# Gated attention mix on one core: score ring of four banks, GpSimd takes sums and reciprocals of branch B, DMA turns the output tiles

## The chip, the cores and the metric

The kernel runs on one core of a Trainium2 chip. A core has a matrix engine (TensorE, PE in the profile), a vector engine (VectorE, DVE), a scalar engine (ScalarE, ACT), a general engine (GpSimd, POOL), a queue engine for transfers (SyncE, SP) and 16 DMA engines. Each engine runs its own list of instructions in order and waits for the others through semaphores. SBUF is the working memory of 128 partitions. PSUM has eight banks, each 128 partitions by 512 fp32 values; matmuls write there. The metric is device microseconds from start to end of one execution.

## The reference

The kernel computes softmax attention A and a linear attention B over the same input of 2048 tokens and 512 features, 32 heads of 16, and mixes them by a gate for each token:

```python
g = sigmoid((x * gate_w).sum(-1, keepdims=True))
# A: softmax attention
scores = einsum("bhqd,bhkd->bhqk", q, k) * 16 ** -0.5
a = reshape(einsum("bhqk,bhkd->bhqd", softmax(scores), v)) @ A_wo
# B: linear attention; q, k, v from B_wqkv
phi(t) = concat([softmax(t @ w_phi), softmax(-(t @ w_phi))])
kv = einsum("bhsf,bhsd->bhfd", phi(k), v);  z = phi(k).sum(s)
b = reshape(phi(q) @ kv / (phi(q) @ z + 1e-6)) @ B_wo
out = g * a + (1 - g) * b
```

All arrays are bf16. The exponentials of A are the bulk: 32 x 2048 x 2048 scores.

## The kernel before

**Tiles.** The scores of A are cut into 2048 tiles (units) of 128 keys by 512 queries of one head. A pack is the same 128 keys for four heads, in the four row strips of PE's array (32 rows each), so four score matmuls can run beside each other. 16 packs make a group: four heads against all keys for one query chunk. Eight groups make a query chunk, and there are four chunks: 32 groups, 512 packs.

**Two ways to take the exponential.** Most units go to ACT (`_exp`, line 978): the score matmuls (`_qk`, `_scores`, line 931) write to a ring of PSUM banks, and one ACTIVATE takes the exponential of several neighbouring banks into slots of the SBUF tensor ET. The ring has `NRING` = 5 banks, used in groups of three and two in turn (`GROUPS`). ET has `NSLOT` = 25 slots. The other units, 452 of 2048, go to DVE (`_vector_batch`): a tile's scores get one of the free PSUM banks, a DVE instruction (line 847) turns them into the bits of an approximate exponential, and in batches of four tiles two further instructions (line 864, on two and on four thousand elements a partition) add constants to the bits, which makes four terms whose sum is a better approximation. `NUMS` says how many units of each of the 32 groups go this way.

**Values.** `_pv` (line 1034) multiplies the exponentials by the values, four heads in four column strips of the array, and adds them up in a PSUM accumulator, one bank for a group; a vector tile needs four such matmuls, one for each term. A column of ones among the values gives the softmax's sum. `_fill` (line 1041) adds matmuls with zero weights that keep the array busy.

**The norm of A.** When a group is complete, `_norm` transposes the accumulator on DVE (line 1055). For each pair of groups it multiplies the sums by the gate (line 1062), takes reciprocals (1064), multiplies on POOL (1067) and transposes back on DVE (1072) into `onTA`, which the output matmuls read. The last two groups are treated one at a time, on DVE alone.

**Branch B.** `_b_pair` handles two tiles of 128 tokens, eight times for keys and eight for queries: project, copy to SBUF, negate (line 1179), a max tree (1181, 1182), subtract (1184), exponential on ACT (1187), a tree of sums (1189 to 1192), reciprocal (1200), multiply (1194). All but the exponential run on DVE. DMA transposes from SP (lines 1243 and 1276) turn the results.

**PSUM.** Five banks belong to the score ring; the other three serve everything else: the accumulators, the projections, the scores of vector tiles, the outputs.

**The order.** Nothing of the order is left to run time. `Plan.order` is a list scheduler in Python: it goes through all operations with an assumed cost for each (`c_act`, `c_dve`, `c_pe` and constants), an assumed delay from one engine to another (`LAT`, `MORE`), the free PSUM banks and due times counted in packs (`prio`, `rel`, `QDUE`, `KDUE`, `VDUE`, `K0`, `SK`, `Q0`, `SQ`, `NDUE`), and writes one list for each engine. `_late` keeps PE from starting other work that would make the next scores late. `rank` puts an operation whose `urgent` time has come first. `port` makes operations that are named in `PORT` and all POOL operations follow one another in the plan; on the chip there is no such wait. `emit` writes the lists with the semaphore waits. So an instruction that is late on the chip holds up whatever stands behind it on its engine.

The lines that a sentence does not say:

```python
GROUPS = (3, 2)
...
deps=self.qks[-1:] + ([self.exps[k - 2]] if k >= 2 else ...     # _qk: two groups back must be read
...
self.ET[:, a % NS:a % NS + n, cols], self.ps[:, a % NR:a % NR + n, cols], ACT.Exp, scale=SCALE   # _exp
```

Of the kernel before, what the change touches and what calls it, by code (L numbers as in the profile page):

```python
# [39 lines left out]
class Op:  # L40
    def __init__(self, eng, fn, cost, name, prio, rel, kind, lat):
        self.eng, self.fn, self.cost, self.name = eng, fn, cost, name
        self.prio, self.rel, self.kind, self.lat = prio, rel, kind, lat
        self.deps = []
        self.users = []
        self.left = 0
        self.need = False
        self.acquire = None
        self.release = None
        self.sem = None  # L50
        self.start = self.end = None
        self.on_commit = None
        self.array = 0.0
        self.filler = 0
        self.pad = False
        self.filled = 0
        self.strips = None
        self.urgent = 1 << 30
        self.held = self.port = False
        self.alone = -99  # L60
        self.group = None


class Plan:
# [3 lines left out]
    MORE = {("ACT", "PE"): 0.09, ("ACT", "DVE"): 0.1, ("DVE", "PE"): 0.022}  # L68
    ENGS = ("PE", "ACT", "DVE", "POOL", "SP")
    LAT = {"PE": 0.215, "ACT": 0.16, "DVE": 0.12, "POOL": 0.12, "SP": 2.2}  # L70
    SWITCH, PASS, STEP = 0.105, 0.2155, 0.004
    SPAN, SHARE, FILL = 2.4, 0.5, 0.2155
    PAD, PADS, OVER = 0.45, 2, 0.2
    SLIP, GAPS, FLOOR = 0, 0.6, 0.44

    def __init__(self):
        self.ops = []
        self.now = -1
        self.free_banks = []
        self.keep = None  # L80
        self.open = None
        self.pad = None
        self.mode = None
        self.strip = [0.0] * 4
        self.n_qk, self.qks, self.exps = 0, (), ()
        self.n_acc = 0
        self.todo = {}
# [19 lines left out]
    def op(self, eng, fn, cost, reads=(), writes=(), deps=(), name="", prio=0.0, rel=-99, kind="full",  # L107
           acquire=None, release=None, lat=None, array=None, strips=None):
# [20 lines left out]
        o.acquire, o.release = acquire, release  # L129
# [7 lines left out]
    def _late(self, end):  # L137

        k = self.n_qk
        if k < 2 or k >= len(self.qks) or any(d.end is None for d in self.qks[k].deps):  # L140
            return False
# [9 lines left out]
    NEAR = 0.2  # L151
    SAME = 16
    OPEN = 99
    HURRY, FREE = 20, 60
    PORT = ("v_step", "b_neg", "b_max", "b_sub", "b_sum", "b_mul", "n_mul", "n_den", "kvbd")
# [30 lines left out]
    def _bank_for(self, o):  # L186

        if o.group is not None and self.todo.get(o.group - 1, 0) > self.OPEN:
            return False
        return len(self.free_banks) > (self.n_acc < 2 and self.keep is not None and self.keep is not o.acquire)  # L190

    def order(self):
# [14 lines left out]
        while left:  # L207
# [74 lines left out]
            if o.acquire is not None:  # L282
                k = min(range(len(self.free_banks)), key=lambda i: self.free_banks[i][1])
                bank, _, ops = self.free_banks.pop(k)
                o.acquire.bank = bank
                o.deps.extend(ops)
            if o.release is not None:
                self.free_banks.append((o.release.bank, self._seen(o, "PE"), [o]))
# [94 lines left out]
class _Kernel:  # L383
    NRING = 5
    GROUPS = (3, 2)
    NSLOT = 25
# [3 lines left out]
    NA, NST, LEAD = 2, 2, 8  # L390
    KEEP = 15
    URGENT, AHEAD, SOON, REST = 5, -(1 << 30), 4, 6
    QDUE, KDUE, VDUE = 24, 17, 8
    P_Q, P_MUL, P_NEG = 1, 1, 0
    GDUE = 26
    VMIN = 12
    ALONE, EARLY = 9, 8
    PVP = 8
# [29 lines left out]
    def _memory(self, ctx):  # L428
# [13 lines left out]
        self.iden = sb("iden", [P, P], BF16)  # L442
# [3 lines left out]
        self.zero = sb("zero", [P, 32], BF16)  # L446
        self.warm = sb("warm", [P, QCH], BF16)
        self.gwb = sb("gwb", [P, 4, P], BF16)
        self.gh = sb("gh", [P, 2, NQC, 16], F32)
# [20 lines left out]
        self.bq = sb("bq", [P, self.NBQ, 2, 2 * D], BF16)  # L470
        self.btree = sb("btree", [P, 32, 8, 4], BF16)
        self.bsum = sb("bsum", [P, P], F32)
        self.brec = sb("brec", [P, P], FP16)
        self.kvacc = sb("kvacc", [P, 2, 260], F32)
# [8 lines left out]
        tiles = [sb(f"vs{k}", [P, 2, 4, QCH], U16) for k in range(self.NST + self.NA)]  # L483
# [5 lines left out]
    def c_act(n):  # L489
        return 0.050 + n * 0.000834  # L490
# [55 lines left out]
    def _consts(self):  # L546
# [25 lines left out]
        op("POOL", lambda e: e.memset(self.zero[:], 0.0), 0.1, writes=[self.b_zero], prio=-75)  # L572
        self.b_wphi0 = B()
# [14 lines left out]
    def _projections(self):  # L588
# [8 lines left out]
        self.b_rinv, self.b_T2 = B(), B()  # L597
        self._warm(9, None)
        op("ACT", lambda e: e.activation(self.bsum[:, 0:1], self.warm[:, 0:1], ACT.Exp), 1.5, reads=[self.b_warm],
           name="table", prio=-48)  # L600
        for j in range(NQC):
            if j == 0:
                for half, banks in enumerate(((3, 4), (None, None))):
# [69 lines left out]
    def _proj_k0(self, half, bank):  # L673
# [4 lines left out]
                   self.c_dve(256), 2 * half - 2.5, -99, "kproj", [self.b_k0[half]], n=256, bank=bank)  # L678

    def _proj_q0(self, half, bank):  # L680
# [4 lines left out]
        for c in range(4):  # L685
# [3 lines left out]
                   acquire=None if c else pool)  # L689
        for side in range(2):  # L690
# [48 lines left out]
    def _proj_v(self, pr, t0):  # L739
# [5 lines left out]
        for tt in range(2):  # L745
# [8 lines left out]
            mm.urgent = 64 * pr + t0 - self.SOON + 2  # L754
# [53 lines left out]
    NUMS = (4, 10, 12, 14, 14, 14, 14, 14, 14, 14, 14, 14, 15, 14, 16, 14, 13, 14, 15, 14, 17, 14, 15, 15, 14, 14, 11, 15, 21, 16, 21, 12)  # L808

    def _plan_vector(self):  # L810
# [5 lines left out]
        batches = [away[k:k + 4] for k in range(0, len(away), 4)]  # L816
# [18 lines left out]
    def _vector_batch(self, number, units, due):  # L835
# [4 lines left out]
        parts, war = [], list(b_va.readers)  # L840
        for j, u in enumerate(units):
# [5 lines left out]
            parts.append(op("DVE", lambda e, j=j, job=job: e.tensor_scalar(  # L847
                va[:, 0, j, :], self._bank(job), SCALE * LOG2E * 128.0, float(ORIGIN), op0=ALU.mult, op1=ALU.add),
                self.c_dve(512), deps=[m] + war, name="v_bits", prio=at, release=job))
            m.urgent = parts[-1].urgent = u // 4 - self.AHEAD  # L850
# [3 lines left out]
            m.on_commit = lambda _, g=g: self.plan.todo.update({g: self.plan.todo[g] - 1})  # L854
        self.last_bits = parts
# [4 lines left out]
        for k in range(4):  # L860
# [9 lines left out]
            for g in sorted({u // (4 * NT) for u in units}):  # L870
# [4 lines left out]
                def run(e, g=g, src=src, ot=ot, v=v, tile=tile):  # L875
                    for j, u in src:
                        ins = self._values(e, ot, g % 8, u // 4 % NT, {u % 4: tile[:, j, :].bitcast(BF16)}, v)
# [8 lines left out]
    def _attention(self):  # L886
# [14 lines left out]
        self.n_step = 0  # L901
        first = sum(self.GROUPS)
# [40 lines left out]
    def _qk(self, a, b, half=None):  # L943
        plan, NR = self.plan, self.NRING
        units = self.mine[a:b]
        cols = slice(0, QCH) if half is None else slice(256 * half, 256 * half + 256)

        def run(e):
            for _ in range(o.filled):
                e.matmul(self.ps[:, a % NR, :], self.kT[:, 0, 0:P], self.kT[:, 0, 0:QCH], start=True, stop=True)  # L950
# [15 lines left out]
        o.pad = k >= 8  # L966
# [18 lines left out]
    def _pv(self, p):  # L985
# [32 lines left out]
        self.pvs.append(o)  # L1018
        if kt == 0:
# [30 lines left out]
    def _norm(self, qc, src, side, last, dst, b_dst, due, job, alone=False):  # L1050
# [6 lines left out]
        if not (side or alone):  # L1057
# [4 lines left out]
        op("DVE", lambda e: e.tensor_tensor(rinv[:, lo:hi], den, h, ALU.mult), 0.23, reads=reads + [self.b_g],  # L1062
           writes=[b_rinv], name="n_den", prio=due)
        op("DVE", lambda e: e.reciprocal(rinv[:, lo:hi], rinv[:, lo:hi]), 0.2 + 0.1 * n, reads=[b_rinv],  # L1064
           writes=[b_rinv], name="n_rec", prio=due)
        spare = self.P_MUL and n == 2
        op("POOL" if spare else "DVE", lambda e: e.tensor_tensor(  # L1067
# [3 lines left out]
        if side == 1:  # L1071
# [4 lines left out]
    NDUE = 26  # L1076
    K0, SK, Q0, SQ = 34.0, 12.0, 214.0, 14.25

    def _branch_b(self):
# [7 lines left out]
        self.b_kvbd, self.b_onB, self.b_rinvB = B(), [B(), B()], [B(), B()]  # L1087
        self.b_phiT = [B() for _ in range(4)]
# [58 lines left out]
    def _b_pair(self, s, t0, due):  # L1147
# [25 lines left out]
        def chain(ops, off, bufs):  # L1173
            for name, cost, fn in ops:
                spare = self.P_NEG and name == "b_neg"
                op("POOL" if spare else "DVE", fn, 1.35 if spare else cost, reads=bufs, writes=bufs, name=name,
                   prio=due + off)
        spread = lambda t: t[:, :, None, :].to_broadcast([P, 32, DH, 4])
        chain([("b_neg", 0.16 + 1024 * 0.00027, lambda e: e.tensor_scalar(both[:, :, 1], both[:, :, 0], -1.0, 0.0,
                                                                         op0=ALU.mult, op1=ALU.add)),  # L1180
# [6 lines left out]
        op("ACT", lambda e: e.activation(flat, flat, ACT.Exp), 1.8, reads=[b], writes=[b],  # L1187
# [3 lines left out]
                                                                       half[:, :, n:2 * n], ALU.add)) for n in (4, 2)]  # L1191
              + [("b_sum", 0.3, lambda e: e.tensor_tensor(last(self.bsum[:]), half[:, :, 0], half[:, :, 1], ALU.add)),
                 ("b_rec", 0.96, self._b_rec),
                 ("b_mul", two(2048), lambda e: e.tensor_tensor(x, x, spread(last(self.brec[:])), ALU.mult))],  # L1194
              2, [b, self.b_tree])
        return slot

    def _b_rec(self, e):
        with self.nc.allow_low_precision(reason="11 bits, each product is rounded to 8"):
            return e.reciprocal(self.brec[:], self.bsum[:])  # L1200
# [47 lines left out]
    def _b_num(self, t, due):  # L1248
# [4 lines left out]
        b_rinv.readers = []  # L1253
        for hf in range(2):
            job = Job()

            def mm(e, hf=hf, job=job):
# [6 lines left out]
            view = self._view17(job)  # L1264
            r = rinv[:, 16 * hf:16 * hf + 16]
# [7 lines left out]
                prio=due - 20, release=job))  # L1273
        b_rinv.readers = list(muls)
# [26 lines left out]
    def _out(self, qc):  # L1301
        op, NT, NQC = self.plan.op, self.NT, self.NQC
        for tt in range(4):
# [5 lines left out]
            if final:  # L1309
                due = self.NPACK  # L1310
                deps = (self.last_bits if tt < 2 else [self.pvs[-1]]) + [w for b in b_onTA[:3] for w in b.writers]
            else:
                deps = [w for b in b_onTA for w in b.writers]
            for x in first:
                x.prio, x.rel = due, due - (6 if not final else 8 if tt < 2 else 0)
                x.deps += deps
            m = first[-1]
# [58 lines left out]
```

## Time and profile before

| | |
|---|---|
| time, median of 3 runs | 772.5 us (772.28 to 772.59) |
| the profiled execution | 772.22 us, its span 770.2 us |
| busy: PE, DVE, ACT, POOL | 747.0, 725.3, 755.1, 57.9 us |
| ACTIVATE of line 978 | 641 (318 of three tiles, 318 of two, five shorter) |
| bits of vector tiles (line 847), steps (line 864) | 452, 226 |
| granted TensorE clock | 1.0 throughout |

The span runs from the first to the last instruction; some 2 us of the time lie around it. A busy share is an average over the span. A group's line names the source line, the engine, the operation, the tile it writes and the one it reads with their sizes, the count, then busy time and mean duration, then the idle time of the engine just before these instructions and what ended it. The chain that ended last goes back from the last instruction, at each step to what released it or to the instruction before it on its engine; in order of time it gives start, length and the number of instructions of a stretch. In the view by time, PE and PEld are matmuls and their weight loads.

### The profile page before, as it was taken

What the parts mean: (1) busy time and instruction counts of PE and PEld (TensorE: products, weight loads), DVE (VectorE), ACT (ScalarE), POOL (GpSimd) and SP (SyncE); (2) the same over time, 40 slices, a digit from 0 to 9 for tenths busy, and PEclk for the clock granted to TensorE, in tenths of its full rate; (3) what the DMA queues carried; (4) which work ended last, traced back from release to release, by engine and by line L of the source; (5) the groups of instructions that cost most, each with busy time, mean ns of one, the idle gap of its engine ahead of it and who ended that gap; (6) DMA issues with size and microseconds to landing.
All of it is one profiled execution on the core that took longest, in us unless ns stands there. A gap on an engine that the chain in (4) does not pass through costs nothing.

```text
span 770.2 us, 16369 instructions
## 1 busy us (share of the span) xinstructions
PE 747.0 (97%) x7126; PEld 231.5 (30%) x7126; DVE 725.3 (94%) x1207; ACT 755.1 (98%) x663; POOL 57.9 (8%) x73
## 2 busy tenths in 40 slices
PE   8999999999999999999999999999999999999998
PEld 4333333322322232222232223222323232322222
DVE  4789999999999999999999999999999999999994
ACT  6999999999999999999999999999999999999996
POOL 3200102000010100001001010000010101010000
PEclk9999999999999999999999999999999999999999
DMA  9510000000000000000111010102001110100000
GB/s 233 124 29 1 2 1 2 1 1 2 1 1 2 1 2 1 1 2 1 29 28 29 21 35 15 42 9 49 8 9 36 32 31 16 35 9 2 1 2 28
DMA packets 46456, 16.79 MB, mean 22 GB/s; under 512 B 40752, under 2 KB 45872, under 8 KB 46384
## 3 DMA queue, kind: packets, MB, share of 16 engines
q1 hardware_dynamic: 44512, 14.97, 9.1%
q8 instruction: 55, 0.90, 0.5%
q10 hardware_dynamic: 1872, 0.79, 0.4%
q14 instruction: 17, 0.14, 0.1%
HBM read 4.21 MB, written 2.10 MB: 8 GB/s over the span
## 4 chain that ended last, share of the span: by engine, by line
ACT 87%; PE 7%; DVE 5%; DMA 1%; SPq 0%; issue 0%
ACT ET L978 83%; ACT bq L1187 4%; PE ps L931 2%; PE ps L1034 2%; PE ps L640 2%; DVE vs L847 2%; DVE vs L864 1%; DMA xT<-in_A_x_dram 1%; DVE WB L1133 0%; DVE bq L1184 0%; PE ps L1041 0%; DVE bq L1160 0%; DVE btree L1182 0%; PE ps L749 0%; DVE ghB L802 0%; SPq L515 0%
## 5 line engine op out<-in xcount | busy, mean ns | idle before, releaser
L978 ACT ACTIVATE ET<-ps 128x1024 bf16<-128x1024 f32 (+2 forms) x641 | 725.7, 1340 | 2.4 <-PE ps L931 2.4
L931 PE MATMUL ps<-qT,kT 32*128 32x512 bf16 (+1 forms) x2053 | 304.9, 383 | 12.8 <-ACT ET L978 8.2
L847 DVE TENSOR_SCALAR vs<-ps 128x512 uint16<-128x512 f32 x452 | 297.4, 681 | 13.6 <-PE ps L931 11.9
L864 DVE TENSOR_SCALAR vs<-vs 128x2048 uint16<-128x2048 uint16 x226 | 214.8, 955 | 0.8
L1034 PE MATMUL ps<-ET,V 128*32 128x512 bf16 x1596 | 196.7, 387 | 0.1
L1034 PE MATMUL ps<-vs,V 128*32 128x512 bf16 x1808 | 179.9, 384 | 2.9 <-DVE vs L864 2.7
L931 PEld LDWEIGHTS ps<-qT,kT 32*128 32x128 bf16 x2053 | 76.9, 91 | 261.0 <-ACT ET L978 187.1
L1034 PEld LDWEIGHTS ps<-ET,V 128*32 128x32 bf16 x1596 | 49.9, 94 | 92.6 <-issue 79.7
L1041 PE MATMUL ps<-kT,zero 128*32 128x512 bf16 x760 | 75.1, 383 | 0.0
L1034 PEld LDWEIGHTS ps<-vs,V 128*32 128x32 bf16 x1808 | 45.1, 95 | 67.7 <-issue 31.3
L640 PE MATMUL ps<-WB,xT 128*128 128x512 bf16 x192 | 56.7, 384 | 0.4 <-DVE WB L1133 0.4
L728 POOL TENSOR_SCALAR qT<-qtmp,mask 128x512 bf16<-128x512 bf16 x30 | 25.6, 865 | 311.2 <-DVE qtmp L723 311.2
L1067 POOL TENSOR_TENSOR T<-T,rinv 128x512 bf16<-128x512 f32 x15 | 16.5, 1102 | 296.7 <-DVE rinv L1064 296.7
L640 PE MATMUL ps<-xT,WA 128*128 128x512 bf16 x120 | 35.8, 384 | 0.0
L1187 ACT ACTIVATE bq<-bq 128x2048 bf16<-128x2048 bf16 x16 | 31.5, 1970 | 0.4 <-DVE bq L1184 0.3
L1055 DVE STREAM_TRANSPOSE T<-ps 128x512 f32<-128x512 f32 x32 | 22.7, 710 | 7.7 <-PE ps L1034 7.2
L1041 PEld LDWEIGHTS ps<-kT,zero 128*32 128x32 bf16 x760 | 19.4, 95 | 18.9 <-issue 13.7
L1160 DVE CAST bq<-ps 128x512 bf16<-128x512 f32 x32 | 21.7, 683 | 2.2 <-PE ps L640 2.2
L640 PEld LDWEIGHTS ps<-WB,xT 128*128 128x128 bf16 x192 | 14.1, 97 | 27.3 <-issue 16.4
L1184 DVE TENSOR_TENSOR bq<-bq,btree 128x2048 bf16<-128x2048 bf16 x16 | 19.8, 1240 | 0.1
L1194 DVE TENSOR_TENSOR bq<-bq,brec 128x2048 bf16<-128x2048 bf16 x16 | 19.6, 1224 | 0.0
L640 PE MATMUL ps<-WoA,onTA 128*128 128x512 bf16 x64 | 18.7, 382 | 0.0
(75 smaller groups left out, 341.2 us busy)
## 6 DMA issues: line engine op xcount, KB each, us to landing
WB<-in_B_wqkv_dram SPq DMA_DIRECT2D x1, 1536.0 KB, 8.7
out_dram<-WB SPq DMA_DIRECT2D x12, 128.0 KB, 1.7
WA<-in_A_wqkv_dram SPq DMA_DIRECT2D x2, 384.0 KB, 4.5
WoB<-in_B_wo_dram SPq DMA_DIRECT2D x1, 512.0 KB, 3.8
WoA<-in_A_wo_dram SPq DMA_DIRECT2D x1, 512.0 KB, 4.8
WA<-in_A_wqkv_dram ACTq DMA_DIRECT2D x2, 128.0 KB, 3.0
WA<-in_A_wqkv_dram ACTq DMA_DIRECT2D x1, 256.0 KB, 4.2
WA<-in_A_wqkv_dram SPq DMA_DIRECT2D x1, 256.0 KB, 5.0
```

Of the source, the lines that this page charges most:

```text
L640: return e.matmul(out, lhs, rhs, start=start, stop=stop)
L728: x = self.plan.op("POOL", lambda e, side=side: e.tensor_scalar(self.qT[:, s0 + side, :], tmp, self.mask[:, side:side + 1], 0.0, op0=ALU.m ...
L847: parts.append(op("DVE", lambda e, j=j, job=job: e.tensor_scalar(va[:, 0, j, :], self._bank(job), SCALE * LOG2E * 128.0, float(ORIGIN), op ...
L864: o = op("DVE", lambda e, k=k, src=src, dst=dst: e.tensor_scalar(dst, src, float(STEPS[k - 1]), None, op0=ALU.add), 0.16 + k * n * QCH * 0 ...
L931: return e.matmul(out[:, cols], self.kT[32 * i:32 * i + 32, cp, kt * TOK:(kt + 1) * TOK], self.qT[32 * i:32 * i + 32, s, cols], start=True ...
L978: o = plan.op("ACT", lambda e: e.activation(self.ET[:, a % NS:a % NS + n, cols], self.ps[:, a % NR:a % NR + n, cols], ACT.Exp, scale=SCALE ...
L1034: ins = e.matmul(self._bank(ot)[32 * i:32 * i + 32, :], v[:, v0:v0 + 32], tile, start=(kt == 0), stop=(kt == self.NT - 1), tile_position=( ...
L1041: ins = e.matmul(self._bank(ot)[32 * i:32 * i + 32, :], self.zero[:], self.kT[:, 0, 0:QCH], start=False, stop=False, tile_position=(0, 32 ...
L1055: t1 = op("DVE", lambda e: e.transpose(T1[:, side].rearrange("p b s -> p (b s)"), src()), 0.735, deps=last, writes=[b_T1[side]], name="n_t ...
L1160: [lambda e, b, k=k: e.tensor_copy(bq[:, k].rearrange("p (g s v) -> p g s v", g=8, s=2)[:, :, 0, :], b.rearrange("p (g v) -> p g v", g=8))],
L1184: + [("b_sub", two(2048), lambda e: e.tensor_tensor(x, x, spread(tree[:, :, 0]), ALU.subtract))],
L1187: op("ACT", lambda e: e.activation(flat, flat, ACT.Exp), 1.8, reads=[b], writes=[b], name="b_exp", prio=due + 1)
```

## The change

The diff touches constants of the plan, `_norm`, `_b_pair` and several helpers. What it does:

- The score ring has four banks and every group two tiles. Four PSUM banks are free for the rest. ET has 24 slots.
- 481 instead of 452 units go to DVE, from pack 4 on (`VMIN`) instead of 12.
- In `_b_pair` the negation, the last two steps of the tree of sums, the total and the reciprocal run on POOL. In `_norm` the reciprocal of a pair could also go there, but `P_REC` is 0, so that it stays on DVE. The new function `_reciprocal` is seven POOL instructions: a first guess from the bits, and two steps of two products and one linear term each.
- In `_norm`, the transpose back of a pair becomes 16 small SBUF to SBUF copies and one DMA transpose, all from SP, through the new tensor T3. The last two groups keep the DVE transpose.
- The plan's costs and delays change: the exponential's cost is 0.0634 + n x 0.000833 us, delays from ACT are shorter, and many due times move. First keys and queries become urgent ahead of the value projections, pads start at the second group, and the last four value products are exempt from `_late`.
- New options that stay off as the constants are set: `PAIRS` (two vector tiles in one instruction), `P_REC`, `P_M` and `P_BMUL` (further work on POOL).

```diff
-    MORE = {("ACT", "PE"): 0.09, ("ACT", "DVE"): 0.1, ("DVE", "PE"): 0.022}
+    MORE = {('ACT', 'PE'): 0.04, ('DVE', 'PE'): 0.022, ('PE', 'DVE'): 0.027}
-    LAT = {"PE": 0.215, "ACT": 0.16, "DVE": 0.12, "POOL": 0.12, "SP": 2.2}
+    LAT = {"PE": 0.215, "ACT": 0.157, "DVE": 0.12, "POOL": 0.12, "SP": 2.2}
-    SPAN, SHARE, FILL = 2.4, 0.5, 0.2155
-    PAD, PADS, OVER = 0.45, 2, 0.2
-    SLIP, GAPS, FLOOR = 0, 0.6, 0.44
+    SPAN, SHARE, FILL = 2.7, 0.5, 0.2155
+    PAD, PADS, OVER = 0.45, 2, 0
+    SLIP, GAPS, FLOOR = 0, 0.7, 0.5
...
-    NEAR = 0.2
-    SAME = 16
-    OPEN = 99
-    HURRY, FREE = 20, 60
+    TAIL = 0.0
+    NEAR = 0.1
+    SAME = 100
+    OPEN = 2
+    HURRY, FREE = 15, 30
...
-    NRING = 5
-    GROUPS = (3, 2)
-    NSLOT = 25
+    NRING = 4
+    GROUPS = (2, 2)
+    NSLOT = 24
+    PACK, PAIRS, PAIR0 = 4, 0, 0
...
-    NA, NST, LEAD = 2, 2, 8
+    NA, NST, LEAD = 2, 2, 6
-    QDUE, KDUE, VDUE = 24, 17, 8
-    P_Q, P_MUL, P_NEG = 1, 1, 0
+    QDUE, KDUE, VDUE = 28, 17, 11
+    P_Q, P_MUL, P_NEG = 1, 1, 1
+    P_REC, P_SUM = 0, 4
+    P_BACK = 1
+    P_M, P_BMUL, CHUNKS = 0, 0, 2
-    VMIN = 12
-    ALONE, EARLY = 9, 8
-    PVP = 8
+    VMIN = 4
+    FAST = 4
+    VSOON = -2
+    PADK = 2
+    ALONE, EARLY = 12, 6
+    PVP = 10
...
-        return 0.050 + n * 0.000834
+        return 0.0634 + n * 0.000833
...
-                   self.c_dve(256), 2 * half - 2.5, -99, "kproj", [self.b_k0[half]], n=256, bank=bank)
+                   self.c_dve(256), 2 * half - 2.5, -99, "kproj", [self.b_k0[half]], n=256, bank=bank,
+                   urgent=3 * half - 99)
...
-        if side == 1:
+        if side == 1 and not alone and self.P_BACK:
+            parts = [lambda e, i=i, c=c: e.dma_start(
+                self.T3[32 * c:32 * c + 32, :, 32 * i:32 * i + 32],
+                T2[32 * i:32 * i + 32].rearrange("p (b c) f -> p c b f", c=4)[:, c]) for i in range(4) for c in range(4)]
+            self.dma("SP", f"mix{due}", parts, cost=0.55 * 16, reads=[b_T2], writes=[self.b_T3], prio=due, lat=2.2)
+            self.dma("SP", f"back{due}", lambda e: e.dma_start(dst.rearrange("p (b t) -> p b t", b=4),
+                                                               self.T3[:].rearrange("p b f -> p (b f)"), transpose=True),
+                     cost=0.6, reads=[self.b_T3], writes=[b_dst], prio=due, lat=3.0)
+        elif side == 1:
...
-    K0, SK, Q0, SQ = 34.0, 12.0, 214.0, 14.25
+    K0, SK, Q0, SQ = 30.0, 11.5, 214.0, 14.5
...
+    def _reciprocal(self, s, guess, tmp, out, reads, bufs, prio):
...
+        do("r_bits", 0.17 + 0.001 * n, lambda e: e.tensor_scalar(
+            high(guess), high(s), -1.0, float(0x7EE0), op0=ALU.mult, op1=ALU.add))
+        for x, y, by, plus in ((guess, r, -1.2011100358638287, 2.192845599791731), (r, out, -1.0, 2.0)):
+            do("r_mul", 0.17 + 0.0019 * n, lambda e, x=x: e.tensor_tensor(t, s, x, ALU.mult))
+            do("r_rest", 0.17 + 0.001 * n, lambda e, by=by, plus=plus: e.tensor_scalar(
+                t, t, by, plus, op0=ALU.mult, op1=ALU.add))
+            do("r_step", 0.17 + 0.0019 * n, lambda e, x=x, y=y: e.tensor_tensor(y, x, t, ALU.mult))
```

## The prediction

> **What bounds the kernel now.** I read the page first (busy time, then the chain that ended last), next the groups by form, next that chain in order of time, and at the end the instructions in two short windows.
>
> ```profile
> PE 747.0 (97%) x7126; PEld 231.5 (30%) x7126; DVE 725.3 (94%) x1207; ACT 755.1 (98%) x663; POOL 57.9 (8%) x73
> ACT 87%; PE 7%; DVE 5%; DMA 1%; SPq 0%; issue 0%
> ```
>
> Three engines look full, but 87% of the chain that sets the end is ACT, nearly all of it the exponential of line 978. PE's figure is soft: a matmul's end is modelled. POOL is nearly empty.
>
> ```profile
> L978 ACT ACTIVATE ET<-ps 128x1536 bf16<-128x1536 f32 x318 | 494.5, 1555 | 0.4 <-PE ps L931 0.3
> L978 ACT ACTIVATE ET<-ps 128x1024 bf16<-128x1024 f32 x318 | 360.8, 1134 | 1.5 <-PE ps L931 1.5
> L847 DVE TENSOR_SCALAR vs<-ps 128x512 uint16<-128x512 f32 x452 | 297.4, 681 | 13.6 <-PE ps L931 11.9
> L864 DVE TENSOR_SCALAR vs<-vs 128x4096 uint16<-128x4096 uint16 x113 | 138.6, 1228 | 0.3
> L864 DVE TENSOR_SCALAR vs<-vs 128x2048 uint16<-128x2048 uint16 x113 | 76.7, 683 | 0.5
> L1041 PE MATMUL ps<-kT,zero 128*32 128x512 bf16 x760 | 75.1, 383 | 0.0
> L728 POOL TENSOR_SCALAR qT<-qtmp,mask 128x512 bf16<-128x512 bf16 x30 | 25.6, 865 | 311.2 <-DVE qtmp L723 311.2
> L1067 POOL TENSOR_TENSOR T<-T,rinv 128x512 bf16<-128x512 f32 x15 | 16.5, 1102 | 296.7 <-DVE rinv L1064 296.7
> L1200 DVE RECIPROCAL brec<-bsum 128x128 f16<-128x128 f32 x16 | 15.1, 945 | 0.1
> L1072 DVE STREAM_TRANSPOSE onTA<-T 128x512 bf16<-128x512 bf16 x16 | 11.2, 701 | 0.0
> ```
>
> The idle time ahead of the 636 full groups is 1.9 us in all: ACT is fed. Neighbouring exponentials overlap, so their mean durations (1555, 1134 ns) overstate them. Their true rate is in the chain:
>
> ```profile
> 481.02 39.76 ACT ET L978 x35
> ...
> 650.07 97.19 ACT ET L978 x86
> ```
>
> 86 instructions are 43 pairs (three tiles, two tiles): 97.19/43 = 2.260 us a pair. 35 are 17 pairs and one more: 39.76 - 17 x 2.260 = 1.34, a group of three, so a group of two adds 0.917. One tile more adds 0.427, and what remains of either is 0.063 for each instruction, whatever its size. Worked out so over the whole trace, ACT loses 4.7 us to waits: 2.5 in the first 15 us, 2.2 in all the rest.
>
> ```profile
> 12.98 0.39 PE L931 MATMUL ps<-qT,kT 32*128 32x512 bf16 x2
> ...
> 13.41 3.28 ACT L978 ACTIVATE ET<-ps 128x1024 bf16<-128x1024 f32 x3 [1.46 <-PE ps L931]
> ```
>
> This is the largest loss: the second half of the first keys was projected behind twelve value matmuls.
>
> **The sum.** The profiled execution took 772.22 us: span 770.2 and 2.0 around it, 0.3 below the median of 772.5.
>
> *Exponentials.* 29 tiles leave ACT: 29 x 0.427 = -12.4 us. Groups of two turn 641 instructions into 786 (four halves at the start, 781 pairs, one single): 145 x 0.063 = +9.1. Together **-3.2 us**, on the path. [...]
>
> *Start.* Keys and queries of the first chunk now go ahead of the value projections, so most of the wait before 13.41 should go (its excess over the group's own rate is 1.57). Against it, ACT has two groups of 512 columns (0.98 us) instead of 768 and 512 (1.4) before it needs the second half of the queries, which is late by its DVE evacuation: some 0.4 back. **-1.2**; ends -1.6 (nothing back) and +0.4 (the wait stays). Next in line is the second chunk's key evacuation, at 12.93; with 14 tiles ahead of it, it is in time.
>
> *Refill.* A group of two can be refilled only while its neighbour runs. Before, every second window was 0.917 and the others 1.343; now all are 0.917. In the short ones of before, the first score matmul began 0.055 us (at best) to 0.36 (19 of 20) after the banks were freed, and some 0.39 is the latest without loss; those groups still ended 1.347 after their neighbour on average against 1.343, 4 ns lost. 782 windows at 4 ns are 3.1 instead of the 2.2 lost now: **+0.9**. Ends: -2.2 (every loss goes) and +8 (the first rival).
>
> *DVE.* Away go branch B's reciprocals (15.1 at line 1200), fifteen transposes of line 1072 (10.5), two steps of the sum and the total (6.6, 4.6, 4.5) and the negation (6.6): 48 us. The norm's product and reciprocal stay, since `P_REC` is 0. 29 tiles add 29 x 0.681 and 29 x (1.228 + 0.683)/4: 34 us. DVE is 14 us lighter of 725, worth nothing on the path itself; it hides the next item. If it is used up, PE's queue stands behind the late tile and ACT behind PE.
>
> *POOL.* No row has a reciprocal of seven steps; line 1067 (two inputs, 1.06 for 512) and line 728 (one input, 0.69 at its fastest) bound it: per pair of branch B, the negation 1.2, the sums 1.06 + 0.55 + 0.3, the steps some 2.2, so 5.3 x 16 = 85 us (an estimate). POOL goes from 58 to some 143 us of 770, with 176 more instructions. As work it is hidden. What counts is what it does to DVE: in the trace, DVE instructions beside POOL's lost 2.3 us in all, against 44 us of POOL work after the loads, so 85 us would cost 4.4 DVE us, inside the 14 gained: **0**. Lower end 0, since it can speed nothing; upper end in the second rival. POOL is one queue: the q masks (line 728) now stand behind chains that wait for DVE, and the largest step of DVE (the max tree) behind POOL's negation. The q projection is due four packs earlier, which covers that; without cover a mask that is 1 us late stalls ACT 1 us, at most 15 times.
>
> *DMA hops.* Instead of a 0.70 us transpose, 16 copies and one DMA transpose. The four gw loads took 1.93 us to issue, so 0.48 each, 7.7 on SP; 1.7 to landing (wphi) and 2.4 (the transposes at line 1276): 12 us. SP is idle almost throughout; the phiT and onTB transposes and stores behind it come up to 8 us later. An onTA tile is wanted only when its query chunk closes, and the last pair keeps DVE: **0**; ends 0 and +2, were the pair before the last late for the final sum.
>
> *End and order.* From the last exponential to the end are 8.0 us: two DVE transposes around the norm, the output matmuls, the store. All stay: **0**, ends -0.5 and +0.5, for the last value matmuls now go first. A wider look-ahead or another order costs only by the waits above. The slot ring (25 to 24) is twelve groups deep: 0.
>
> Sum: 770.2 - 3.2 - 1.2 + 0.9 = 766.7, and 2.0: **768.7 us** (0.5% faster).
>
> **Rivals.**
>
> *PE becomes the bound (slower).* A visit to the scores is one pass and two changes of the array's mode:
>
> ```profile
> 300.40 0.39 PE L931 MATMUL ps<-qT,kT 32*128 32x512 bf16 x2
> 300.72 1.05 PE L1041 MATMUL ps<-kT,zero 128*32 128x512 bf16 x16
> ```
>
> 16 filler matmuls are four passes, (1.05 - 0.39)/3 = 0.22 each; from 300.40 to 300.72 is a pass and 0.10 for one change. So a visit costs 0.42, and 145 more cost 61 us; the 29 tiles add 29 value passes, 6 us. What PE can give: fillers, 190 passes x 0.22 = 42, and waiting, 43 over the trace by the array's own idle time less the changes. For it: 67 of 85, and between 120 and 160 us fillers and waiting together are only 1.3 of 40 where some 3.5 more would be wanted. Against: a group of two leaves two of the four row strips to a vector tile's scores, so passes are saved, and a fourth free bank lets projections move. If ACT pays the part that the fillers do not cover and some two thirds of the idle time cannot be used (67 - 42 - 15 = 10 us), 768.7 - 0.9 + 10 = **778**. It decides once a group of two takes 6 ns over 0.917 on average ((3.2 + 1.2 us)/782).
>
> *DVE and POOL block each other.* For it: line 728 takes 0.69 alone and 1.73 at its longest, and four of the 4096 steps of line 864 beside POOL lost 0.86 us together. DVE spends some 45% of its time in such steps and in two-input operations; if every POOL us beside one were lost, 85 x 0.45 = 38 us, 24 beyond the 14 gained, and some 20 of DVE's 45 idle us lie between start and end: 4 us reach ACT, **773**. [...]
>
> *The gain is eaten.* The start stays as it is, or the fixed part per exponential is more than 0.063: at 0.085 (12.4/145) the move gives nothing. Time 771 to 774, say **772**. [...] The chain above speaks against it.
>
> **How the numbers follow.** The forecast has 0.58, the eaten gain 0.12, PE 0.22, the lock 0.08 (773 is within 0.2% of before; half of its chance counts as slower). 0.2% (1.5 us) is about what a measurement of this kernel tells from no change. So faster 0.58, same 0.16, slower 0.26. The forecast's own range is 765.0 (768.7 - 0.9 - 2.2 and the ends of the start) to 770.9. For 8 in 10 the upper end takes in the lock and PE's stated price: 765 to 778.5.
>
> **What would show it.** Right: 786 exponentials, a pair's rate of 0.917 in long unbroken stretches of the chain, no wait near 13 us, fewer fillers, PE still below full, DVE busy near 711 plus a few. Wrong: breaks of the chain at the scores, most between 40 and 160 us; long rows of line 864's successor beside POOL; an exponential of branch B that waits for DVE.

## The result and the profile after

| | before | changed |
|---|---|---|
| time, median | 772.48 us (6 runs, 772.22 to 773.18) | 778.50 us (6 runs, 776.34 to 780.00) |
| ratio | | 1.0074, 95% interval 1.0057 to 1.0090 |
| the profiled execution, its span | 772.22, 770.2 us | 778.40, 776.6 us |
| exponentials of A on ACT | 641 | 786 |
| mean granted TensorE clock | 1.000 | 0.991 |

The kernel is 0.7% slower where 0.5% faster was forecast. The page of the changed kernel, its busy times, the granted clock by slices, and the chain that ended last:

```profile
PE 745.3 (96%) x7027; PEld 219.4 (28%) x7091; DVE 716.8 (92%) x1157; ACT 752.9 (97%) x808; POOL 187.9 (24%) x252
...
PEclk9999999999999999999999999999999999997999
...
ACT 70%; PE 20%; DVE 5%; DMA 3%; SPq 1%; issue 1%
```

ACT's share of the chain fell from 87% to 70%; that of DMA rose from 1% to 3% and that of SP's queue from 0 to 1%. One slice of the clock reads 7, which no slice of the kernel before does. The groups by form have the exponential (line 978 is now line 1038) and the bits of the vector tiles (847 is 897):

```profile
L1038 ACT ACTIVATE ET<-ps 128x1024 bf16<-128x1024 f32 x781 | 721.8, 1141 | 10.4 <-PE ps L990 10.0
...
L897 DVE TENSOR_SCALAR vs<-ps 128x512 uint16<-128x512 f32 x481 | 309.1, 679 | 24.0 <-PE ps L990 22.2
...
L1104 PE MATMUL ps<-kT,zero 128*32 128x512 bf16 x648 | 63.8, 385 | 0.0
```

Idle time ahead of the full exponentials went from 1.9 to 10.4 us, behind the scores of line 990. But the chain in order of time has stretches without any break:

```profile
127.51 61.42 ACT ET L1038 x67
...
527.49 45.83 ACT ET L1038 x50
```

61.42/67 = 0.917 and 45.83/50 = 0.917: the rate that the prediction took for a group of two, held over 67 groups. PE refills a ring of four banks in time. So ACT is not slowed evenly; it is stopped at a few places. With each exponential's end set against the end of the one before it and the group's own rate, ACT loses 14.2 us (4.7 before), and 11.0 of them between 381 and 386, at 438, 479 and 619, and between 700 and 710 us. The waits of PE name what stopped it there:

```profile
PE ps L1361 <- DMA phiT<-bq: 3.0, 2, 1.6
...
PE ps L674 <- DMA WT<-onB: 2.1, 2, 1.1
...
PE ps L990 <- DMA onTA<-T: 1.4, 1, 1.4
```

Five waits for a DMA that SP issues; the kernel before has no wait for any of these three tensors in this view. SP's own instructions before the first and the last of the five, by time:

```profile
366.39 10.92 SPq L1141 DMA_DIRECT2D T<-T  x16
377.35 2.70 SPq L1343 DMA_TRANSPOSE phiT<-bq  x2
380.10 1.27 SPq L1145 DMA_TRANSPOSE onTA<-T  x1
```

```profile
684.48 11.20 SPq L1141 DMA_DIRECT2D T<-T  x16
695.72 2.69 SPq L1343 DMA_TRANSPOSE phiT<-bq  x2
```

The sixteen copies of a hop hold SP for 11 us, 0.69 each, and branch B's transposes start in the moment when the last copy is issued. What follows on PE and ACT, by time, around the first:

```profile
378.74 0.60 PE L1097 MATMUL ps<-vs,V 128*32 128x512 bf16 x4
380.10 1.27 SPq L1145 DMA_TRANSPOSE onTA<-T  x1
...
380.72 0.30 PE L1361 MATMUL ps<-kvbd,phiT 128*128 128x68 bf16 x4 [1.38 <-DMA phiT<-bq]
...
381.38 1.02 ACT L1038 ACTIVATE ET<-ps 128x1024 bf16<-128x1024 f32 x1 [1.19 <-PE ps L990]
...
384.00 1.04 PE L1097 MATMUL ps<-vs,V 128*32 128x512 bf16 x5
...
384.11 1.03 ACT L1038 ACTIVATE ET<-ps 128x1024 bf16<-128x1024 f32 x1 [0.49 <-PE ps L990]
```

PE stands in its queue at branch B's product with phiT; the next scores are behind it, and ACT is behind the scores. The wait is over at 380.7, yet ACT goes on losing at 384. The stages say why; the columns are stretch, length, busy time of PE, weight loads, DVE, ACT and POOL with counts, then the granted clock and two figures of the DMA engines:

```profile
378.00:381.60 3.60, 2.23 (x28) 0.60 (x22) 2.26 (x4) 2.41 (x4) 0.00 (x0) 1.00 0.85 159
381.60:385.00 3.40, 3.40 (x30) 0.64 (x23) 3.21 (x7) 2.73 (x3) 0.00 (x0) 0.51 0.15 31
...
699.00:709.00 10.00, 9.59 (x63) 2.53 (x68) 6.59 (x18) 6.41 (x7) 0.00 (x0) 0.50 0.27 54
```

After two of the waits (1.38 us at 379 and 1.65 at 697) the array's clock is halved, for 3.4 and for 10.2 us; after one of 1.36 us, for onTA at 617, and the two of 1.0 to 1.1 it is not. At half the clock PE did not refill two banks in 0.917 us: in the second stretch ACT is busy 6.4 of 10 us. Of the 11.0 us, some 5.8 fall on the first exponential after each wait and 5.0 on the later ones within the halved clock.

### The profile page after: what moved, and what is told of

It is laid out like the page before. It is cut to its first block, busy times and chain, and to the rows that moved or that the text cites. A ratio compares the mean times of both kernels' runs of the same rounds, so it can differ in the third digit from the quotient of the medians.

```text
span 776.6 us, 16787 instructions
## 1 busy us (share of the span) xinstructions
PE 745.3 (96%) x7027; PEld 219.4 (28%) x7091; DVE 716.8 (92%) x1157; ACT 752.9 (97%) x808; POOL 187.9 (24%) x252
## 4 chain that ended last, share of the span: by engine, by line
ACT 70%; PE 20%; DVE 5%; DMA 3%; SPq 1%; issue 1%
ACT ET L1038 66%; PE ps L990 7%; PE ps L1097 7%; ACT bq L1265 3%; PE ps L674 2%; DVE vs L897 2%; SPq L1141 1%; PE ps L1104 1%; PE ps L785 1%; DVE vs L922 1%; DMA phiT<-bq 1%; DMA xT<-in_A_x_dram 1%; DMA WT<-onB 1%; DVE WB L1211 1%; PE ps L1361 0%
## 5 line engine op out<-in xcount | busy, mean ns | idle before, releaser
L1038 ACT ACTIVATE ET<-ps 128x1024 bf16<-128x1024 f32 (+1 forms) x786 | 724.6, 1138 | 11.2 <-PE ps L990 10.7
L897 DVE TENSOR_SCALAR vs<-ps 128x512 uint16<-128x512 f32 x481 | 309.1, 679 | 24.0 <-PE ps L990 22.2
L990 PE MATMUL ps<-qT,kT 32*128 32x512 bf16 (+1 forms) x2052 | 312.6, 386 | 13.4 <-ACT ET L1038 8.0
L922 DVE TENSOR_SCALAR vs<-vs 128x2048 uint16<-128x2048 uint16 (+2 forms) x242 | 229.9, 963 | 0.8
L1097 PE MATMUL ps<-vs,V 128*32 128x512 bf16 x1924 | 215.2, 388 | 0.8 <-issue 0.5
L1268 POOL TENSOR_TENSOR btree<-btree 128x512 f16<-128x512 f16 (+1 forms) x32 | 35.4, 1106 | 206.4 <-DVE btree L1267 205.2
L1104 PE MATMUL ps<-kT,zero 128*32 128x512 bf16 x648 | 63.8, 385 | 0.0
L674 PE MATMUL ps<-WB,xT 128*128 128x512 bf16 x163 | 49.0, 383 | 2.7 <-issue 2.2
L1256 POOL TENSOR_SCALAR bq<-bq 128x1024 bf16<-128x1024 bf16 x16 | 18.4, 1149 | 57.0 <-DVE bq L1238 42.4
L802 POOL TENSOR_SCALAR V<-V 128x544 bf16<-128x544 bf16 x16 | 12.0, 750 | 37.3 <-DVE V L795 36.9
```

Source lines behind the costliest of these rows:

```text
L674: return e.matmul(out, lhs, rhs, start=start, stop=stop)
L897: bits = lambda e, to, src: e.tensor_scalar(to, src, SCALE * LOG2E * 128.0, float(ORIGIN), op0=ALU.mult, op1=ALU.add)
L922: o = op("DVE", lambda e, k=k, src=src, dst=dst: e.tensor_scalar(dst, src, float(STEPS[k - 1]), None, op0=ALU.add), 0.16 + k * n * QCH * 0 ...
L990: return e.matmul(out[:, cols], self.kT[32 * i:32 * i + 32, cp, kt * TOK:(kt + 1) * TOK], self.qT[32 * i:32 * i + 32, s, cols], start=True ...
L1038: o = plan.op("ACT", lambda e: e.activation(self.ET[:, a % NS:a % NS + n, cols], self.ps[:, a % NR:a % NR + n, cols], ACT.Exp, scale=SCALE ...
L1097: ins = e.matmul(self._bank(ot)[32 * i:32 * i + 32, :], v[:, v0:v0 + 32], tile, start=(kt == 0), stop=(kt == self.NT - 1), tile_position=( ...
```

## The experiments

Theory H: the hops' copies hold SP, the transposes behind them come late, PE's queue stands, and the clock adds to it. Rival R: PE has no slack left with groups of two, and any disturbance shows there (the prediction's first rival). Rival L: POOL and DVE block each other (its second).

**One copy for sixteen.** The clearest test keeps all five orders and shortens only SP's time.

```diff
-            parts = [lambda e, i=i, c=c: e.dma_start(
-                self.T3[32 * c:32 * c + 32, :, 32 * i:32 * i + 32],
-                T2[32 * i:32 * i + 32].rearrange("p (b c) f -> p c b f", c=4)[:, c]) for i in range(4) for c in range(4)]
+            parts = [lambda e: e.dma_start(
+                self.T3[:].rearrange("p b f -> p (b f)"),
+                T2[:].rearrange("p b s -> p (b s)"))]
```

> The changed kernel with one copy of the whole tile in place of the 16 small ones; it leaves out the rearrangement, so the output tiles of A are in a wrong order. All five lists of instructions keep their order, and the transposes that followed the copies still do. Theory H: SP is free some 10 us earlier at each hop, the five waits of PE for a DMA go, the clock stays at 1.000, and ACT loses 14.2 - 11.0 = 3.2 us: 778.5 - 11.0 = 767.5. Rival R: the order is the same and just as tight, so the losses come at the scores instead: 774 or more.

767.12 us, ratio 0.9930 (0.9915 to 0.9945): 11.4 us less than the changed kernel, with every other instruction in its place. SP by time, where the changed kernel's first wait was, and the same stage late in the run:

```profile
366.05 0.47 SPq L1141 DMA_DIRECT2D T<-T  x1
374.61 2.62 SPq L1343 DMA_TRANSPOSE phiT<-bq  x2
```

```profile
699.00:709.00 10.00, 9.88 (x106) 2.71 (x103) 10.00 (x15) 10.00 (x12) 0.00 (x0) 1.00 0.02 3
```

The transposes start 2.4 us earlier, counted from the start of the copies, when their data is ready. No wait of PE for branch B's or the norm's DMA is left in its view, the clock is 1.00 and ACT is busy 10.00 of 10. It loses 3.6 us in the whole run. As causes of the slowdown, rivals R and L both fall with this run: groups of two, 481 vector tiles and all of POOL's work are in it.

**One hop of fifteen.** As the run before, but the hop of the last but one pair keeps its sixteen copies (`if due != 449.0:` around the one copy).

> As the run with one copy in place of sixteen (the rearrangement is left out, so the output tiles of A are in a wrong order), but the hop of the last but one pair, the one that held SP from 684 to 696 us in the changed kernel, keeps its sixteen. Theory H (each hop costs what the transposes behind it then cost PE, and nothing else): 767.1 and what that place lost in the changed kernel, 5.4 us, of which the bare wait is 1.9 and the halved clock 3.5: 772.5; if the halved clock is only a matter of how long the array idles and in which window, anything from 769.0 to 772.5. All other places stay without a wait. Rival (the loss is spread over all fifteen hops): 767.1 + 11.0/15 = 767.9.

Median 772.72 us of ten runs, 769.05 to 774.16 (ratio 0.9994, 0.9982 to 1.0005). The profiled execution is the shortest, 769.05:

```profile
core 0: 767.2 us, clock 1.000
```

```profile
PE ps L1363 <- DMA phiT<-bq: 1.6, 1, 1.6
```

There the wait of 1.6 us came and the clock stayed; ACT lost 1.6 us at that place and the time is 1.9 over the one-copy run: the bare wait. The other nine runs have a lower mean clock, and their times follow it: 0.996 in those of 771.37 and 771.72, 0.993 in six of 772.50 to 773.01, 0.991 in that of 774.16. A stretch of 3.4 us at half the clock takes 1.7/769 = 0.0022 off the mean, so by this estimate they had two, three and four such stretches, the profiled run none, and each adds about 1.3 us ((774.16 - 769.05)/4). Only the shortest run was traced, so where these stretches lie is not shown. The same hop, in the same order of work, thus costs 2 us at a mean clock of 1.000 and 4 to 7 at 0.996 to 0.991. The median is 5.6 over the one-copy run: theory H's 772.5, where the rival expected 767.9.

**No hops.** `P_BACK = 0`: the DVE transpose back, ordered anew.

> The changed kernel with the DVE transpose back in place of the 16 copies and the DMA transpose; the planner orders everything anew. Theory H (the 16 copies hold SP for 11.0 us, so the transposes queued behind them land late, PE's queue stands on them, and twice the TensorE clock halves): no wait of PE for phiT, onB or onTA, clock 1.000 except in the last microseconds, and the 11.0 us that ACT loses at those five places go (0.8 to 5.4 us each): 778.5 - 11.0 = 767.5, give or take 2 since the order is new. Rival R (PE has no slack left with groups of two, and would stall at any disturbance): DVE gets 10.5 us more work and no time is won, 776 or more, with waits of the exponentials for the scores spread over the run.

785.24 us, ratio 1.0163 (1.0148 to 1.0178): a plain miss for theory H. Rival R's time (776 or more) is met, but not its mechanism: of what ACT loses, 7.0 us fall on one place and the tail is 7.2 us longer. No wait for those DMAs is left; by time the largest loss and the tail read:

```profile
686.16 0.62 PE L1097 MATMUL ps<-vs,V 128*32 128x512 bf16 x8 [1.72 <-DVE vs L922]
...
689.54 1.94 ACT L1038 ACTIVATE ET<-ps 128x1024 bf16<-128x1024 f32 x2 [6.21 <-PE ps L1097]
...
770.15 0.74 DVE L922 TENSOR_SCALAR vs<-vs 128x512 uint16<-128x512 uint16 x2
...
776.49 0.72 DVE L1118 STREAM_TRANSPOSE T<-ps 128x512 f32<-128x512 f32 x1 [5.59 <-PE ps L1097]
```

DVE is behind. ACT waits 6.2 us for value matmuls that wait for a vector tile's steps; PE's own waits there are 1.72 and 0.59 us, and from 687.5 to 690.9 the clock is halved, so part of the 6.2 is the clock again. DVE works on tiles until 770.9, 2.5 us after the last exponential; the tail is 15.1 us instead of 7.9. The reading is that 481 tiles need the 10.5 us that the hops take from DVE; the next run tests it. So undoing one part alone gave DVE too much, and the numbers of tiles had to be chosen again for each plan, as in three of the later runs.

**No hops, tiles chosen anew.** `P_BACK = 0` and 476 tiles.

> No hops, the DVE transposes back, and the numbers of vector tiles chosen anew for that plan (476 in all). The first run without hops took 785 because 481 tiles were too many for a DVE with 10 us more work: DVE finished its last steps 2.4 us after the last exponential and the tail was 15.1 us. Theory H': with tiles that DVE can do, the wait of 6.3 us at 689 and the long tail go; ACT has six tiles more than with 482, 6 x 0.458 = 2.7 us, so 769 to 772. If the hops were the only reason for the gain of the one-copy run, and DVE is not what limits: 767.

771.02 us, ratio 0.9985 (0.9970 to 1.0000); tail 7.9, losses 5.1 us. With DVE able to follow, the 14 us are gone, and against the kernel before the difference is hardly clear of noise. Nine of the ten runs lie between 770.56 and 771.28; one took 776.44, at a mean clock of 1.000, and why is open.

**The hops with SP's true costs.** The plan counts 0.70 us for a copy and 1.35 for a transpose.

```diff
-cost=0.55 * 16, reads=[b_T2]
+cost=0.70 * 16, reads=[b_T2]
...
-transpose=True), cost=0.6,
+transpose=True), cost=1.35,
```

> The changed kernel with the hops kept, but the plan is given what SP took in its profile: 0.70 us a copy instead of 0.55 and 1.35 us a DMA transpose instead of 0.6; the order is planned anew. Theory H: the hops themselves are harmless once the plan knows that SP is held, so no wait of PE for a DMA over 0.3 us, clock 1.000, 766 to 770. If the hops hurt in another way than by lateness (DMA traffic, SP's own waits), 774 or more. Rival R: 775 or more.

Median 771.69 us (ratio 0.9988, 0.9979 to 0.9998), just above the 770 expected. PE has no wait for those DMAs any more, so lateness was the harm. What is left is the tail, 10.6 us: DVE ends its last tile step 0.1 us after the last exponential, where in the changed kernel it is done 8.4 us before it. The profiled execution is the longest of eleven (776.03) and can be read for order only: its mean clock is 0.993, which makes some 11 us at half the clock (0.007 x 774.2/0.5, an estimate), and 1.000 in the ten others, and it is 4.3 us over the median.

**The same, tiles chosen anew (482).**

> The hops kept with all sixteen copies, the plan given 0.70 us a copy and 1.35 us a transpose as in the run with SP's true costs, and the numbers of vector tiles for the 32 groups chosen anew for that plan (482 in all), since that run lost 2.7 us in its tail (10.6 against 7.9 us) to vector tiles planned past the last exponential. Theory H: a tail of 7.9, no wait of PE for a DMA, losses of 3 to 5 us: 766 to 769. If the hops cost something beside lateness: 771 or more.

767.71 us, ratio **0.9934** (0.9922 to 0.9946): faster than both kernels, 1.4% below the changed one, and it computes the whole reference. Its SP by time shows the same sixteen copies with the transposes still behind them:

```profile
364.00 10.96 SPq L1141 DMA_DIRECT2D T<-T  x16
375.00 2.70 SPq L1343 DMA_TRANSPOSE phiT<-bq  x2
```

PE comes to phiT only at 381.2 there, since the plan knew. The full exponentials:

```profile
L1038 ACT ACTIVATE ET<-ps 128x1024 bf16<-128x1024 f32 x781 | 720.6, 1141 | 1.5 <-PE ps L990 1.0
```

**POOL's part undone.** The last kernel with negation, sums and reciprocal back on DVE and 476 tiles chosen for it.

> The replanned kernel with hops, but branch B's negation, sums and reciprocal are back on DVE (48 - 10.5 = 37.5 us of DVE by the rows of the kernel before, less what neighbours overlap), and the numbers of vector tiles chosen anew (476 in all). Theory H (POOL's part is a relief of DVE and disturbs it by a few us at most): six tiles more on ACT, 6 x 0.458 = 2.7 us, 770 to 772 against 767.7. Rival (POOL and DVE block each other so that the relief is worth nothing): 766 to 768. If POOL's part alone made the change's gain: 774 or more.

770.39 us, ratio 0.9975 (0.9964 to 0.9986). POOL's part is worth 2.7 us beside the hops, by the six tiles it lets DVE take. DVE instructions that ran beside POOL's took some 6 us in all over the median of their shape's other instructions in the replanned kernel and some 3 here: DVE's instructions were slower beside POOL's, at a price far below the relief.

**The ring alone.** The kernel before with four banks, groups of two and 24 slots, and another bank for one of the first projections; 452 tiles stay.

> The kernel before with a ring of four banks, groups of two and 24 slots, and nothing else: 452 tiles stay with DVE. ACT gets 800 instead of 641 exponentials: 159 x 0.063 = +10.0 us. Theory H (refilling groups of two costs next to nothing, 4 ns a group): 772.5 + 10.0 and 0 to 3 more, 782.5 to 785.5. Rival R (PE can't refill in 0.917 us): 790 or more, with waits of the exponentials for the scores.

784.99 us, ratio 1.0164 (1.0148 to 1.0179), as expected. The profiled execution is the longest of four (786.34), 14.1 us over that of the kernel before. 10.0 us are the 159 instructions. Of the rest, 1.9 are more loss in the start and 2.8 one stretch in which the clock is halved:

```profile
300.00:308.00 8.00, 6.01 (x56) 1.71 (x56) 7.93 (x15) 8.00 (x9) 0.00 (x0) 1.00 0.01 2
308.00:315.50 7.50, 6.27 (x44) 1.23 (x45) 5.76 (x10) 5.27 (x6) 0.00 (x0) 0.54 0.00 0
```

That stretch begins in the longest wait of PE in its view, for a bank that ACT has yet to read:

```profile
PE ps L950 <- ACT ET L978: 6.2, 11, 2.7
```

From 305.95 to 307.86 ACT takes an exponential of branch B, and with four banks PE has work for a part of that time only: it stands from 306.5 to 309.2. In most other stretches of 40 us ACT loses 0.2 us or less. So the small ring makes ACT issue more and, behind the start, starves it at one place, through the clock.

## Why the prediction was wrong, point by point

**The step that failed is the term for the DMA hops, put at 0 with an end of +2.** The runs show +11.4: 778.50 against 767.12 with nothing else changed. The step named the mechanism, that the phiT and onTB transposes behind the copies come later, and then asked only who waits for onTA. It did not ask who waits for phiT and onB: PE, in order, ahead of the scores. And onTA, put at nothing, was waited for once, 1.4 us at 617, where ACT lost 1.1. It also took 0.48 us a copy from four small loads; these copies take 0.69 each, so SP is held 11 us and not 7.7. The views of the kernel before could not warn: they have no wait of PE for phiT, onB or onTA, and SP had little else to issue then. The plan's own constants, 0.55 a copy and 0.6 a transpose against 0.69 and 1.2 to 1.35, stood in the kernel; with the measured ones put in, PE's waits for these DMAs are gone.

**The clock was not in the prediction at all.** It nearly doubled the price of the hops: 5.0 of the 11.0 us that ACT loses at those places fall in the two stretches of halved clock after the wait is over. In the run with one hop it took 3.7 of the median price of 5.6. It also spreads the times: the six runs of the changed kernel have mean clocks of 0.993 (776.34, 777.00), 0.991 (778.40, 778.61, 778.93) and 0.988 (780.00), in the order of their times, about as three, four and five stretches of 3.4 us would have it by the estimate above (0.993, 0.991 and 0.989).

**Exponentials: -3.2, right.** 786 of them at the rates taken make the sum over ACT's whole list 746.7 us against 750.0, and long stretches run at 0.917. The rival by which each instruction costs more than 0.063 falls.

**Start: -1.2, half right.** The wait of 1.57 is gone; losses in the first 40 us are 1.5 to 1.8 us (changed and one-copy kernel) against 2.5, so -0.7 to -1.0. A loss of 0.9 at 86 us (0.4 at 84 in the kernel before), which the point on POOL explains, took about half of it back.

**Refill: +0.9, over-estimated.** Away from start and tail and the DMA places, ACT loses 0.02 us or less in most stretches of 40. In the one-copy run all losses together are 3.6 against 4.7. The rival in which PE becomes the bound is refuted: that run has the same PE list. What the prediction had held against this rival came about: line 1104 has 648 fillers instead of 760, and the visits to the scores rose from 672 to 780, by 108 and not by 145, since 786 groups and 481 vector tiles share the 780. That the time met its price, 778, is chance: it came by another mechanism.

**DVE and POOL: right in sign, POOL under-sized.** DVE went from 725.3 to 716.8 (711 forecast). POOL went to 187.9, not 143: the added rows are longer than their bound, 1.15 us for the sum of 512 at best and up to 2.06, and 2.8 us for the seven steps, each at its fastest. DVE instructions beside POOL lost some 6 us by the count above, where 4.4 were estimated. Nearly all of it stayed hidden, but not the whole: in the one-copy run a small DVE copy (line 838) beside POOL's negation took 0.91 us, PE then waited 0.68 us for a vector tile, and ACT lost 0.9 at 86 us. In the run with POOL's part undone the same copy took 0.17 and ACT lost 0.15 there. So the slowing that the second rival named is there, but cost the path about 0.8 us and not 4; that one engine stands still while the other works, the lock of the forecast's chances, no run shows.

**End: 0, right** for the changed kernel (8.0 to 7.9 us); it is where plans with too many vector tiles lose (15.1 and 10.6).

With the hops' term at 0 the sum gives 768.7, and the one-copy run, in which the hops cost nothing that shows, took 767.1: the other terms were near. The range's lower end adds up to 765.2 from the terms that are named for it, not 765.0, and the terms of its upper end, 770.9, are not given; the result lies far outside either way.

## What to carry to other kernels

A transfer queue was an engine here, held 11 us by sixteen copies: when many small issues are put on one, list what else it issues in that time, and who stands in order behind the arrival of each. A plan's assumed issue times should be set against a trace before its order is trusted; here 0.15 us a copy and 0.75 a transpose, with the vector tiles chosen anew, decided between 0.7% slower and 0.7% faster. And a part of a balanced schedule can't be undone alone: without the hops the same number of vector tiles took 785 us, with five fewer 771.

## What the runs showed of the hardware that was not expected

Ahead of the tail the TensorE clock was halved for 3.41 us and for 10.24, three times as long (changed kernel, from 381.64 and from 699.07 us, at 0.50 in both), for 3.4 (no hops, from 687.5) and for some 6.9 (ring alone, an estimate from 0.54 over 7.50 us: 2 x 0.46 x 7.50). The length of PE's wait alone did not decide whether it came. It came after waits of 1.38 and 1.65 us (changed kernel, 379 and 697 us), of 1.72 (no hops, 684) and during one of 2.7 (ring alone, 307). It did not come after 1.36 (changed kernel, 617), after 1.0 to 1.1 (436 and 477), nor after 1.6 in the traced run with one hop.

PE's busy time over 3.41 us did not decide it alone either. In the 3.41 us that ended where the clock fell, PE was busy 2.04 and 1.76 us (changed kernel, 381.64 and 699.07); in those from 615.27 it was busy 2.03, and the clock stayed at 1.00. What decides is not shown.

In the changed kernel a small copy between partitions of SBUF (8 KB) held SP for 0.69 us (10.92 and 11.20 for sixteen), a DMA transpose behind the copies for 1.27 (onTA) to 1.35 (phiT, 2.70 for two).
